# Linear attention and a GELU layer on one core: loads issued as slots come free, x in token order with whole-tile stores, and one step fewer transposed by DMA

## The chip, the cores and the metric

One core of a Trainium2 chip runs the whole program. The metric is the time on the device in microseconds (us); for the kernel before, three timed runs are shown, and one further execution was profiled. TensorE (PE) multiplies matrices, VectorE (DVE), ScalarE (ACT) and GpSimd (POOL) do elementwise work, and SyncE (SP) issues nearly all DMAs, one after the other, from one queue.

## The reference

The first half is block-wise linear attention with a decay lam per head: q, k and v are (4, 8, 768, 64), that is batch, heads, tokens and head width. The second half takes the attention's output as x, 3072 tokens by 512, through a layer with a tanh GELU.

```python
for b in range(nb):                      # blocks of 64 tokens
    intra = einsum('bhic,bhjc->bhij', qb, kb) * Dmask     # lam**(i-j) for i >= j, else 0
    intra = einsum('bhij,bhjd->bhid', intra, vb)
    inter = einsum('bhid,bhde->bhie', qb * lam_pow, kv_state)
    out[:, :, sl] = intra + inter
    kv_state = lam_block * kv_state + einsum('bhsd,bhse->bhde', kb * rev_pow, vb)
x = out.transpose(0, 2, 1, 3).reshape(3072, 512)
h = x @ w_in                             # 512 x 2048
g = 0.5 * h * (1 + tanh(c * (h + 0.044715 * h**3)))
return g @ w_out                         # 2048 x 512
```

## The kernel before

**Steps.** The attention is cut into 24 steps. A pair of steps covers 256 tokens of one batch entry (a super block, `sb`, three for each batch entry), and each step of the pair covers four of the eight heads. Inputs and weights are cast to fp16 on the chip.

**Loads.** `load_step(s)` (L60) issues three loads of 256 KB each, of q, k and v, from the SyncE queue (L67). Partition p of a tile holds the tokens 2p and 2p + 1, next to each other, so a load moves long rows. The tiles come from a pool of five slots for each of q, k and v; a load waits until the cast of an older step has freed a slot. At the top of the program the steps 0 to 3 are put on the queue, then the weights (L78, L84), mixed with steps 4 and 5, then steps 6 to 11. From step 8 of the loop on, `load_ahead(n + 4)` adds one step at a time.

**Casts.** `prep(s)` (L180) multiplies q by its decay on DVE (L195), casts k on ACT (L200) and multiplies v by the inverse decay on POOL (L201). The attention needs q and k with the head width on partitions. Up to step 7 TensorE transposes them, in `stage_t(s)`: eight products with an identity (L217) into PSUM, and a copy out of it (L221 on ACT for steps 1 to 3, else L223 on DVE). From step `FIRST_DMA_T` on, `prep` issues a DMA transpose instead (L205), on SyncE's queue too, and `stage_t` does nothing.

**Regions.** `region(n, s)` (L235) is TensorE's part of the attention. For step n it makes the scores (Sps, L255) and the products of k and v that feed the state (L268); DVE multiplies the scores by the mask (PT, L289). For step s = n - 1 it adds the masked scores times v (L304) and the state times q (L314), in PSUM (OK). ACT then copies the result into xT (L322), which holds x transposed: channels on partitions, tokens along the row. `update` makes the new state on DVE (L341, L344) and a block-diagonal copy of it on POOL (u, L348).

In PSUM the 128 columns of one half (c) of a super block stand as j, t: first the tokens of one parity, then those of the other, because a partition held two neighbouring tokens. xT keeps that order. A token tile of the second half's output therefore comes out with partitions 0 to 63 for the even rows and 64 to 127 for the odd ones, and it is stored in two pieces:

```python
for j in range(2):
    pin(nc.sync.dma_start(out=dst[j], in_=o32[half64(j), :]))
...
return out[row0 : row0 + P, :].rearrange("(p j) e -> j p e", j=2)
```

**The second half** is cut into pieces, which `queue_group(g)` (L361) puts on a list, `filler`. `mm1` multiplies xT by w_in (Hps, L373, four or eight products with four passes over the channels) and ACT applies the GELU (gT, L375). `mm2` multiplies gT by a quarter of w_out (O2ps, L384, four products of 512 columns); after the fourth quarter DVE copies the tile to SBUF (L391) and SyncE stores it (L393). There are seven groups of one or two super blocks. `fill(n)` takes n pieces off the list, so that TensorE has work between the regions. `mm2_last` makes the last tile, in two column ranges, and stores them from SyncE and ACT (L410).

**Order.** `pin` keeps the instructions of each engine in the order of the program text; that order is written out by hand. Up to step 7 it is a list of calls (L449 to L509), afterwards a loop. `idle(n)` (L426) issues n products of 128 by 512 on ones whose result nobody reads. The waits between engines follow from the tiles that they share.

Of the kernel before, what the change touches and what calls it, by code (L numbers as in the profile page):

```python
# [15 lines left out]
def kernel(  # L16
# [10 lines left out]
    nc = tc.nc  # L27
# [8 lines left out]
    NF = DFF // P  # L36
    NC = DM // P
    NSTEP = B * NSB * 2
    FIRST_DMA_T = 8
    PSUM = bass.MemoryType.PSUM  # L40

    const = ctx.enter_context(tc.tile_pool(name="const", bufs=1))
# [71 lines left out]
    load_wout(2)  # L114
    load_wout(3)
    load_step(5)
    for s in range(6, 12):
        load_step(s)

    def load_ahead(s):  # L120
# [35 lines left out]
    def square(i):  # L156
        pin(nc.vector.tensor_tensor(sq[i + 1][:], sq[i][:], sq[i][:], ALU.mult))
# [22 lines left out]
    def prep(s):  # L180
        half = s % 2
        q32, k32, v32 = ld32.pop(s)
        hs = slice(half * HH, (half + 1) * HH)

        def wide(t):
            return t.rearrange("p j h d -> p h j d")

        def decay(t):
            return t[:, hs, :].unsqueeze(3).to_broadcast([P, HH, 2, D])

        tqk = a16p.tile([P, 2, 2, HH, D], FP16, tag="qk16", name=f"qk16_{s}")
        tq, tk = tqk[:, 0], tqk[:, 1]
        tv = a16p.tile([P, 2, HH, D], FP16, tag="v16", name=f"v16_{s}")
        q_eng = nc.gpsimd if s == 3 else nc.vector
        pin(q_eng.tensor_tensor(wide(tq), q32[:], decay(dq), ALU.mult))  # L195
        if s == 0:
            inverse(halves[0])
            odd(halves[1])
            inverse(halves[1])
        pin(nc.scalar.activation(out=wide(tk), in_=k32[:], func=AF.Copy))  # L200
        pin(nc.gpsimd.tensor_tensor(wide(tv[:]), v32[:], decay(dv), ALU.mult))  # L201
        a16[s] = (tq, tk, tv)
        if s >= FIRST_DMA_T:
            o = qkp.tile([P, 2, 2, 2, P], FP16, tag="qkT", name=f"qkT_{s}")
            pin(nc.sync.dma_start_transpose(out=o[:].rearrange("p a j h t -> p (a j h) t"),  # L205
                                            in_=tqk[:].rearrange("p a j h d -> p (a j h d)")))
            qkT[s] = o

    def stage_t(s):
        if s >= FIRST_DMA_T:  # L210
# [21 lines left out]
    def half64(i):  # L232
        return slice(64 * i, 64 * i + 64)

    def region(n, s, split=False):  # L235

        OK = [ps_M.tile([P, 512], FP32, tag="M", name=f"OK{c}") for c in range(2)]
        opened = set()

        def start(c, hl):  # L240
            if (c, hl) in opened:
                return False
            opened.add((c, hl))
            return True

        if n is not None:
            o = qkT[n]
            _, tk, tv = a16[n]
            Sps = ps_S.tile([P, 2, 2, 2, P], FP32, tag="S", name="Sps")

            def scores():
                for hp in range(2):
                    for jk in range(2):
                        for hl, c in TILES:
                            pin(nc.tensor.matmul(  # L255
                                Sps[half64(c), hl, hp, jk, :],
                                o[half64(hl), 1, jk, hp, half64(c)],
                                o[half64(hl), 0, :, hp, half64(c)], start=True, stop=True,
                                skip_group_check=True))

            def products():
                last = (n // 2) % NSB == NSB - 1
                for jk in range(2):
                    for hp in range(2):
                        for c, hl in TILES:
                            if c == 1 and last:
                                continue
                            pin(nc.tensor.matmul(  # L268
                                OK[c][half64(hl), 256 + hp * D : 256 + hp * D + D],
                                tk[half64(c), jk, 2 * hp + hl, :],  # L270
                                tv[half64(c), jk, 2 * hp + hl, :],
                                start=start(c, hl), stop=(jk == 1), skip_group_check=True))
                Kps[n] = OK

            if split:
                products()
                update(n, 0)
                scores()
            else:
                scores()  # L280
                products()
            PT = []
            for hps in ([slice(0, 1), slice(1, 2)] if split else [slice(0, 2)]):
                w = hps.stop - hps.start
                t = ptp.tile([P, 2, w, 2, P], FP16, tag=f"PT{w}", name=f"PT_{n}_{hps.start}")
                for src, dst in ([(Sps[:, :, hps.start], t[:, :, 0])] if split else
                                 [(Sps[:].rearrange("p a b c d -> p (a b) c d"),
                                   t[:].rearrange("p a b c d -> p (a b) c d"))]):
                    pin(nc.vector.tensor_tensor(  # L289
                        dst.rearrange("p a c d -> p a (c d)"),  # L290
                        src.rearrange("p a c d -> p a (c d)"),
                        mask[:].unsqueeze(1).to_broadcast([P, 2 * w, 2 * P]), ALU.mult))
                PT += [t[:, :, i] for i in range(w)]
            PTs[n] = PT
        if s is None:
            return
        sbg, half = divmod(s, 2)
        o = qkT.pop(s)
        PT = PTs.pop(s)
        _, _, tv = a16.pop(s)  # L300
        for hp in range(2):
            for jk in range(2):
                for c, hl in TILES:
                    pin(nc.tensor.matmul(  # L304
                        OK[c][half64(hl), hp * P : hp * P + P], tv[half64(c), jk, 2 * hp + hl, :],
                        PT[hp][half64(c), hl, jk, :], start=start(c, hl), stop=False,
                        skip_group_check=True))
        ins = ins_of.pop(s)
        for c in range(2):
            u = ins[c]  # L310
            if u is None:
                continue
            for hp in range(2):
                pin(nc.tensor.matmul(OK[c][:, hp * P : hp * P + P], u[:, hp].rearrange("p l d -> p (l d)"),  # L314
                                     o[:, 0, :, hp, half64(c)], start=False, stop=True,
                                     skip_group_check=True))
        g, i = group_of[sbg]
        if g not in xT:
            xT[g] = xtp.tile([P, NC, len(groups[g]) * SB], FP16, tag="xT", name=f"xT_{g}")
        dst = xT[g][:, 2 * half : 2 * half + 2, i * SB : (i + 1) * SB]  # L320
        for c in range(2):
            pin(nc.scalar.activation(  # L322
                out=dst[:, :, c * P : (c + 1) * P],
                in_=OK[c][:, 0:256].rearrange("p (hp m) -> p hp m", hp=2), func=AF.Copy))

    ins_of = {}

# [33 lines left out]
    def queue_group(g):  # L361
# [18 lines left out]
        def mm2(tau, part):  # L380
            if part == 0:
                O2[tau] = ps_M.tile([P, DM], FP32, tag="M", name="O2ps")
            for f in range(4 * part, 4 * part + 4):
                pin(nc.tensor.matmul(O2[tau][:], gT[:, f, tau * P : (tau + 1) * P],  # L384
                                     w_out16[:, f, :], start=(f == 0), stop=(f == NF - 1)))
            if part < 3:
                return
            o2 = O2.pop(tau)
            dst = rows(tau)
            o32 = otp.tile([P, DM], FP32, tag="o32", name="o32")  # L390
            pin(nc.vector.tensor_copy(out=o32[:], in_=o2[:]))  # L391
            for j in range(2):
                pin(nc.sync.dma_start(out=dst[j], in_=o32[half64(j), :]))  # L393

        def rows(tau):
            row0 = groups[g][0] * SB + tau * P
            return out[row0 : row0 + P, :].rearrange("(p j) e -> j p e", j=2)

        def mm2_last(tau):
            dst = rows(tau)  # L400
            o32 = otp.tile([P, DM], FP32, tag="o32", name="o32")
            for lo, hi in ((0, 384), (384, DM)):
# [4 lines left out]
                                         stop=(f == NF - 1)))  # L407
                pin(nc.vector.tensor_copy(out=o32[:, lo:hi], in_=o2[:]))
                for j, eng in ((0, nc.sync), (1, nc.scalar)):
                    pin(eng.dma_start(out=dst[j][:, lo:hi], in_=o32[half64(j), lo:hi]))  # L410

        for f in range(0, NF, per):
            filler.append(lambda f=f: mm1(f))
# [18 lines left out]
    def fill(n):  # L432
        for _ in range(min(n, len(filler))):
            filler.pop(0)()
# [14 lines left out]
    idle(12)  # L449
    prep(0)  # L450
    stage_t(0)
    square(5)
    square(6)
    prep(1)
# [1 line left out]
    idle(2)  # L456
    R(0, None)
    stage_t(1)
    idle(2)
    U(0)  # L460
    prep(2)
    R(1, 0)
    stage_t(2)
    idle(3)
    U(1)
# [23 lines left out]
    prep(5)  # L489
    fill(4)  # L490
    stage_t(5)
    fill(2)
    R(5, 4)
    U(5)
    prep(6)
    fill(2)
    stage_t(6)
    fill(2)
    R(6, 5)
    U(6)  # L500
    prep(7)
    fill(2)
    stage_t(7)
    prep(8)
    fill(2)
    R(7, 6)
    U(7)
# [3 lines left out]
    for n in range(8, NSTEP + 1):  # L511
        m = n if n < NSTEP else None
        if m is not None:
            load_ahead(n + 4)
            stage_t(n)
        if n + 2 < NSTEP:
            prep(n + 2)
# [39 lines left out]
```

## Time and profile before

| | |
|---|---|
| timed runs | 222.67, 221.65, 222.20 us, median 222.2 |
| profiled execution | 219.72 us, of which the span from first to last instruction is 217.9 |
| TensorE busy | 205.9 us (94%), 2105 products |
| DVE, ACT, POOL busy | 91.7, 91.8, 64.9 us |
| mean granted TensorE clock | 0.981 |
| DMA | 38.08 MB, mean 175 GB/s |
| SyncE's issues | 72 loads of 256 KB, 8 of weights, 46 stores of 128 KB, 16 transposes |

The page cuts the span into 40 equal slices of 5.45 us; a digit is the busy share of an engine in that slice, in tenths, and for PEclk the clock that TensorE was granted. The chain of work that ended last is followed back from the last instruction, at each step to what released it. The groups give, for a line and an operation, the count, the busy time and the mean duration, and the idle time of the engine ahead of them with what ended it.

### The profile page before, as it was taken

To read this page: it belongs to the slowest core of one execution; us is meant where nothing else is said; L and a number is where in the kernel's file an instruction comes from. 1 tells how busy PE (TensorE), PEld (TensorE's weight loads), DVE (VectorE), ACT (ScalarE), POOL (GpSimd) and SP (SyncE) were. 2 spreads that over 40 slices of the span, in tenths; PEclk is the share of its full clock that TensorE was granted. 3 is DMA by queue.
4 is the path that set the end of the run, shared out by engine and by line. 5 is a ranking of instruction groups with operands and counts; after the bars stand their busy time and mean duration, and the time that the engine had idled before them with its cause. 6 is when DMAs were issued, how large, how long until landed. Compare 5 with 4: busy or idle time off the path is not lost.

```text
span 217.9 us, 5061 instructions
## 1 busy us (share of the span) xinstructions
PE 205.9 (94%) x2105; PEld 107.6 (49%) x2105; DVE 91.7 (42%) x178; ACT 91.8 (42%) x175; POOL 64.9 (30%) x82
## 2 busy tenths in 40 slices
PE   7699999999939999999999999999999999999993
PEld 2264444555825686444454544544554454444452
DVE  4778612587722642634526621445730251100121
ACT  2375665323823266177701277620377310466000
POOL 5494146634724432124224203403410110000000
PEclk9969999999979999999999999999999999999998
DMA  5999999999989869499943969744330023200223
GB/s 139 300 335 390 385 345 376 288 297 294 293 190 241 146 168 250 114 228 195 293 101 77 225 183 215 183 96 101 79 70 0 0 51 78 68 3 0 46 50 96
DMA packets 63303, 38.08 MB, mean 175 GB/s; under 512 B 19120, under 2 KB 56240, under 8 KB 63280
## 3 DMA queue, kind: packets, MB, share of 16 engines
q1 hardware_dynamic: 63120, 37.63, 67.5%
q8 instruction: 16, 0.26, 0.5%
q10 hardware_dynamic: 160, 0.13, 0.2%
q14 instruction: 7, 0.06, 0.1%
HBM read 27.27 MB, written 6.29 MB: 154 GB/s over the span
## 4 chain that ended last, share of the span: by engine, by line
PE 86%; DMA 4%; POOL 3%; DVE 2%; ACT 2%; SPq 1%; issue 1%; DVEq 0%; POOLq 0%
PE Hps L373 38%; PE O2ps L384 35%; PE Sps L255 4%; PE OK L314 3%; DMA v<-in_v_dram 3%; PE OK L304 3%; PE O2ps L405 2%; DMA qkT<-qk 2%; PE Tps L217 1%; POOL u L348 1%; SPq L67 1%; PE OK L268 1%; POOL v L201 1%; DVE PT L289 1%; DVE qk L195 1%
## 5 line engine op out<-in xcount | busy, mean ns | idle before, releaser
L373 PE MATMUL Hps<-xT,w_in 128*128 128x512 f16 (+1 forms) x448 | 86.5, 351 | 0.2 <-ACT xT L322 0.2
L384 PE MATMUL O2ps<-w_out,gT 128*128 128x512 f16 x368 | 82.9, 379 | 0.0
L375 ACT ACTIVATE gT<-Hps 128x512 f16<-128x512 f32 x96 | 57.2, 597 | 36.4 <-PE Hps L373 35.5
L373 PEld LDWEIGHTS <-w_in 128*128 128x128 f16 x448 | 43.8, 99 | 38.3 <-issue 0.5
L348 POOL TENSOR_TENSOR u<-t,lumask 128x256 f16<-128x256 f32 x40 | 28.7, 728 | 97.7 <-DVE t L344 66.0
L384 PEld LDWEIGHTS <-gT 128*128 128x128 f16 x368 | 35.4, 98 | 39.7
L289 DVE TENSOR_TENSOR PT<-Sps,mask 128x1024 f16<-128x1024 f32 (+1 forms) x25 | 29.4, 1180 | 50.4 <-PE Sps L255 50.4
L322 ACT ACTIVATE xT<-OK 128x256 f16<-128x256 f32 x48 | 15.9, 381 | 59.8 <-PE OK L314 43.3
L391 DVE COPY o<-O2ps 128x512 f32<-128x512 f32 x23 | 15.8, 690 | 53.5 <-PE O2ps L384 50.7
L201 POOL TENSOR_TENSOR v<-v,dv 128x512 f16<-128x512 f32 x24 | 25.8, 1079 | 3.8 <-DMA v<-in_v_dram 2.3
L195 DVE TENSOR_TENSOR qk<-q,dq 128x512 f16<-128x512 f32 x23 | 20.4, 893 | 6.3 <-DMA q<-in_q_dram 6.3
L200 ACT ACTIVATE qk<-k 128x512 f16<-128x512 f32 x24 | 14.9, 626 | 7.1 <-DMA k<-in_k_dram 7.1
L344 DVE SCALAR_TENSOR_TENSOR t<-t,lamu,OK 128x64 f32<-128x64 f32 x64 | 14.5, 275 | 1.6 <-PE OK L268 0.6
L255 PE MATMUL Sps<-qkT 64*64 64x128 f16 x384 | 10.4, 228 | 4.8 <-DMA qkT<-qk 3.5
L255 PEld LDWEIGHTS <-qkT 64*64 64x64 f16 x384 | 6.4, 110 | 14.4 <-issue 7.0
L304 PE MATMUL OK<-PT,v 64*64 64x128 f16 x384 | 10.7, 226 | 0.0
L430 PE MATMUL idle<-ones 128*128 128x512 f16 x25 | 8.7, 488 | 1.5 <-DVE ones L126 1.5
L103 POOL CAST w_out<-wo 128x1024 f16<-128x1024 f32 x6 | 6.6, 1115 | 10.6 <-DMA wo<-in_moe_w_out_dram 10.6
L314 PE MATMUL OK<-qkT,u 128*128 128x128 f16 x80 | 8.8, 226 | 0.0
L268 PE MATMUL OK<-v,qk 64*64 64x64 f16 x320 | 7.3, 196 | 0.8 <-POOL v L201 0.8
L304 PEld LDWEIGHTS <-v 64*64 64x64 f16 x384 | 7.2, 112 | 0.9 <-issue 0.8
L217 PE MATMUL Tps<-ident,qk 128*128 128x128 f16 x64 | 5.9, 232 | 1.3 <-DVE qk L195 0.6
(34 smaller groups left out, 51.1 us busy)
## 6 DMA issues: line engine op xcount, KB each, us to landing
q<-in_q_dram SPq DMA_DIRECT2D x24, 256.0 KB, 4.5
k<-in_k_dram SPq DMA_DIRECT2D x24, 256.0 KB, 4.7
v<-in_v_dram SPq DMA_DIRECT2D x24, 256.0 KB, 5.1
out_dram<-o SPq DMA_DIRECT2D x46, 128.0 KB, 2.4
wi<-in_moe_w_in_dram SPq DMA_DIRECT2D x4, 1024.0 KB, 10.2
wo<-in_moe_w_out_dram SPq DMA_DIRECT2D x4, 1024.0 KB, 8.8
qkT<-qk SPq DMA_TRANSPOSE x16, 3.9
out_dram<-o SPq DMA_DIRECT2D x1, 96.0 KB, 2.1
```

Of the source, the lines that this page charges most:

```text
L195: pin(q_eng.tensor_tensor(wide(tq), q32[:], decay(dq), ALU.mult))
L201: pin(nc.gpsimd.tensor_tensor(wide(tv[:]), v32[:], decay(dv), ALU.mult))
L255: pin(nc.tensor.matmul(Sps[half64(c), hl, hp, jk, :], o[half64(hl), 1, jk, hp, half64(c)], o[half64(hl), 0, :, hp, half64(c)], start=True, ...
L289: pin(nc.vector.tensor_tensor(dst.rearrange("p a c d -> p a (c d)"), src.rearrange("p a c d -> p a (c d)"), mask[:].unsqueeze(1).to_broadc ...
L304: pin(nc.tensor.matmul(OK[c][half64(hl), hp * P : hp * P + P], tv[half64(c), jk, 2 * hp + hl, :], PT[hp][half64(c), hl, jk, :], start=star ...
L314: pin(nc.tensor.matmul(OK[c][:, hp * P : hp * P + P], u[:, hp].rearrange("p l d -> p (l d)"), o[:, 0, :, hp, half64(c)], start=False, stop ...
L322: pin(nc.scalar.activation(out=dst[:, :, c * P : (c + 1) * P], in_=OK[c][:, 0:256].rearrange("p (hp m) -> p hp m", hp=2), func=AF.Copy))
L348: pin(nc.gpsimd.tensor_tensor(bd[:], t[:].unsqueeze(2).to_broadcast([P, 2, 2, D]), lumask[:, 2 * half : 2 * half + 2, :].unsqueeze(3).to_b ...
L373: pin(nc.tensor.matmul(Hps[:, i, :], w_in16[:, c, f * P : (f + 1) * P], x[:, c, :], start=(c == 0), stop=(c == NC - 1)))
L375: pin(nc.scalar.activation(out=gT[:, f0 : f0 + per, :], in_=Hps[:], func=AF.Gelu_apprx_tanh))
L384: pin(nc.tensor.matmul(O2[tau][:], gT[:, f, tau * P : (tau + 1) * P], w_out16[:, f, :], start=(f == 0), stop=(f == NF - 1)))
L391: pin(nc.vector.tensor_copy(out=o32[:], in_=o2[:]))
```

## The change

- `FIRST_DMA_T` goes from 8 to 9: step 8 is transposed on TensorE and copied out by DVE, steps 9 to 23 by DMA.
- At the top only steps 0 to 8 are loaded. From step 6 on, `prep(s)` ends with the loads of step s + 3, behind its casts and its transpose; the loop's own `load_ahead(n + 4)` goes.
- ACT writes xT in token order: it reads j, t from PSUM and writes t, j. The rows of an output tile are then 128 neighbouring rows, and a tile is one store of 256 KB. In `mm2_last` each of the four stores takes 64 neighbouring rows.
- `prep(6)`, `prep(7)` and `prep(8)` stand earlier in the list of calls, and three calls of `idle` are added or made longer, five products in all.

```diff
-    FIRST_DMA_T = 8
+    FIRST_DMA_T = 9
...
-    for s in range(6, 12):
+    for s in range(6, 9):
         load_step(s)
...
             qkT[s] = o
+        if s >= 6:
+            load_ahead(s + 3)
...
             pin(nc.scalar.activation(
-                out=dst[:, :, c * P : (c + 1) * P],
-                in_=OK[c][:, 0:256].rearrange("p (hp m) -> p hp m", hp=2), func=AF.Copy))
+                out=dst[:, :, c * P : (c + 1) * P].rearrange("p hp (t j) -> p hp j t", j=2),
+                in_=OK[c][:, 0:256].rearrange("p (hp j t) -> p hp j t", hp=2, j=2),
+                func=AF.Copy))
...
-            for j in range(2):
-                pin(nc.sync.dma_start(out=dst[j], in_=o32[half64(j), :]))
+            pin(nc.sync.dma_start(out=dst, in_=o32[:]))
...
-            return out[row0 : row0 + P, :].rearrange("(p j) e -> j p e", j=2)
+            return out[row0 : row0 + P, :]
...
-                    pin(eng.dma_start(out=dst[j][:, lo:hi], in_=o32[half64(j), lo:hi]))
+                    pin(eng.dma_start(out=dst[half64(j), lo:hi], in_=o32[half64(j), lo:hi]))
...
     stage_t(0)
+    idle(1)
...
     stage_t(1)
-    idle(2)
+    idle(5)
     U(0)
     prep(2)
     R(1, 0)
+    idle(1)
     stage_t(2)
...
     stage_t(5)
+    prep(6)
     fill(2)
     R(5, 4)
     U(5)
-    prep(6)
     fill(2)
     stage_t(6)
+    prep(7)
     fill(2)
     R(6, 5)
     U(6)
-    prep(7)
-    fill(2)
+    fill(1)
+    prep(8)
+    fill(1)
     stage_t(7)
-    prep(8)
     fill(2)
     R(7, 6)
...
         if m is not None:
-            load_ahead(n + 4)
             stage_t(n)
```

## The prediction

> **What bounds the kernel now.** I read the head of the page first, then its slices, then a table of stages, then the chain of work that ended last.
>
> ```profile
> span 217.9 us, 5061 instructions
> PE 205.9 (94%) x2105; PEld 107.6 (49%) x2105; DVE 91.7 (42%) x178; ACT 91.8 (42%) x175; POOL 64.9 (30%) x82
> PE   7699999999939999999999999999999999999993
> PEclk9969999999979999999999999999999999999998
> ```
>
> TensorE is busy 94% of the span and no other engine passes 49%, so only time in which TensorE idles or runs slowed can be won. The slices (5.45 us each) show where that is: the first two, the twelfth (3 tenths, about 60 us, the clock down to 7 behind it) and the last. The table of stages gives sizes (stretch, its length, busy time of PE, PEld, DVE, ACT and POOL, granted clock, DMA share, GB/s).
>
> ```profile
> 60.00:63.46 3.46, 0.00 (x0) 0.00 (x0) 0.00 (x0) 0.56 (x1) 1.50 (x2) 0.91 0.86 180
> 63.46:70.90 7.44, 7.44 (x86) 4.71 (x90) 2.84 (x6) 2.42 (x5) 2.63 (x3) 0.81 1.05 233
> 70.90:214.40 143.50, 143.50 (x1384) 73.14 (x1384) 51.75 (x91) 59.01 (x116) 28.37 (x36) 1.00 0.52 116
> ```
>
> From 70.90 to 214.40 TensorE never idles, at clock 1.00: nothing that the change does to loads and stores there can help, it can only hurt. The hole from 60.00 to 63.46 and the lower clock behind it are what can be won. The chain in order of time (start, length, work) says what the hole is:
>
> ```profile
> 53.15 0.62 PE Tps L217 x8
> ...
> 55.52 0.35 PE Sps L255 x16
> ...
> 56.43 3.51 PE Hps L373 x32
> 60.05 3.37 DMA qkT<-qk
> 63.46 0.64 PE Sps L255 x15
> ...
> 65.08 2.37 PE Hps L373 x16
> 67.45 3.45 PE O2ps L384 x16
> ```
>
> TensorE waits for the DMA transpose of step 8, the first one made by DMA. Why that starts only at 60.05 is read from SyncE's queue, DVE and ACT:
>
> ```profile
> 53.43 0.78 SPq L67 DMA_DIRECT2D v<-in_v_dram  x1
> 54.26 5.61 SPq L393 DMA_DIRECT2D out_dram<-o  x8
> 60.05 2.77 SPq L205 DMA_TRANSPOSE qkT<-qk  x2
> 54.41 0.70 DVE L195 TENSOR_TENSOR qk<-q,dq 128x512 f16<-128x512 f32 x1
> 51.53 1.15 ACT L200 ACTIVATE qk<-k 128x512 f16<-128x512 f32 x2
> ```
>
> These casts are step 8's q (done at 54.41 + 0.70 = 55.11) and the k of steps 7 and 8 (done at 52.68). The transpose could have gone at 55.1. It stood behind the last of the twelve loads that are put on the queue at the top, and behind eight half-tile stores.
>
> **The change, part by part.**
>
> *Step 8 back on TensorE (FIRST_DMA_T 9).* The hole goes:
>
> ```profile
> PE Sps L255 <- DMA qkT<-qk: 3.5, 1, 3.5
> PE Tps L217 <- DVE qk L195: 0.4, 1, 0.4
> ```
>
> Minus 3.5 us (first row; the columns are total, times, longest). With it goes the half clock behind it. A region and the 16 Hps products after it take 63.46 to 67.45, 3.99 us. The same region at 55.52 was through at 56.43, 0.91, and 16 of the 32 Hps products there take 1.75: 2.66 together. So minus 1.3 us. In exchange TensorE makes eight transposes, 0.62 us by the row of 53.15: plus 0.6. DVE copies their result out of PSUM (0.69 us, the 43.10 row below) while TensorE has the two filler pieces, 16 Hps products or 1.75 us, that `fill(2)` puts between `stage_t(8)` and the scores: nothing on the path, and 0.7 if that cover were gone.
>
> *`prep` of steps 6, 7 and 8 moved forward.* Each is a cast on DVE (q), ACT (k) and POOL (v), and DVE's order decides.
>
> ```profile
> 43.10 0.69 DVE L223 COPY qkT<-Tps 128x1024 f16<-128x1024 f16 x1 [1.30 <-PE Tps L217]
> 45.43 1.22 DVE L289 TENSOR_TENSOR PT<-Sps,mask 128x1024 f16<-128x1024 f32 x1
> 46.94 0.68 DVE L195 TENSOR_TENSOR qk<-q,dq 128x512 f16<-128x512 f32 x1
> 52.38 0.72 DVE L195 TENSOR_TENSOR qk<-q,dq 128x512 f16<-128x512 f32 x1
> 57.86 1.74 DVE L195 TENSOR_TENSOR qk<-q,dq 128x512 f16<-128x512 f32 x2
> L67 SPq DMA_DIRECT2D k<-in_k_dram x1: 1927/1927/1927, 38.2 to 38.2; - x1
> DMA to landing us min/median/max: 6.1/6.1/6.1
> DMA to landing us min/median/max: 3.1/4.9/9.4
> ```
>
> q6 goes from 46.94 to behind the copy at 43.10, so DVE reaches it at 43.8. Its load must be there: k6 was issued at 38.2 and landed 6.1 later (the first two figures of landing are this one load and all loads), at 44.3, and q6 stands one place ahead of it. It runs before PT at 45.43, for which 0.9 us stay. The copy of step 6 then has one cast less ahead of it than before. q7 goes from 52.38 to behind that copy, and q8 takes its place at 52.38; the store's copy (0.69) and the copy of step 7 follow, done at 54.5 for scores at 55.52 - 0.4 = 55.1: 0.6 to spare. q9 ends 0.4 before 58.73 (half of the last DVE row), the copy of step 8 about 59.0; the scores of step 8 come at 63.46 - 3.5 - 0.4 + 0.6 = 60.2. So none waits. The gain is the wait of step 7's transposes for their own q cast, the second wait row above: minus 0.4, since that cast now lies a step ahead. What it costs if q6's load takes the longest landing seen, 9.4 in place of 6.1: 3.3 less the 1.5 us of room just named (0.9 and 0.6), 1.8.
>
> *Loads.* SyncE meets loads 9, 10 and 11 one `prep` at a time, the last two behind three stores. Each load is now issued three steps ahead of its cast, 22 us at the 7.44 of the stage table, where the slowest landed in 9.4: nothing. In the loop it stands behind the step's transpose instead of ahead of it; TensorE waits for neither there: nothing.
>
> *Stores.* 23 whole stores in place of 46 halves, which took 0.70 each (5.61 for eight). A whole one costs SyncE between 0.70 and two halves, 1.40; a 256 KB load took 0.78, so near the lower end: four of them about 3. Off the path, and 2.5 us earlier for what follows on the queue, with 0 as the other bound. The stores after the last product keep number and size: nothing.
>
> *Step 9's transpose* is what is late next. Its queue is free about 57.5 (60.05 less 2.5), its q cast ends about 58.3, and its scores come at 70.90 - 4.6 = 66.3 if the sum below holds. The transposes of this trace landed in (least, median, longest):
>
> ```profile
> DMA to landing us min/median/max: 3.0/3.9/6.1
> L322 ACT ACTIVATE xT<-OK 128x256 f16<-128x256 f32 x48 | 15.9, 381 | 59.8 <-PE OK L314 43.3
> L169 DVE COPY lumask<-sq 64x4 f32<-64x4 f32 x2 | 0.3, 160 | 0.0
> L170 DVE TENSOR_TENSOR lamu<-lumask 128x4 f32<-128x4 f32 x1 | 0.2, 162 | 0.0
> ```
>
> So it is there between 61.3 and 64.4: in time by 1.9 us at worst.
>
> *xT in token order.* The 48 copies on ACT (381 ns each) will write every second element. No ACT row of this trace writes so. The nearest, though far off, is DVE's copy into every second element of lumask, 160 ns, against 162 for an operation as wide without gaps. I take 381 unchanged. Bounds: 0 and a doubling. A doubled pair, 1.5 us, would still lie under the eight O2ps products (half of 3.45, 1.73) that follow the region ahead of every group but the first, and show there alone, 0.8 us. [...]
>
> *Five more idle products* (1, 3 and 1) in the opening.
>
> ```profile
> 14.89 1.01 POOL qk L195
> 11.29 0.42 PE L255 MATMUL Sps<-qkT 64*64 64x128 f16 x16 [0.68 <-ACT qkT L221]
> 11.70:15.00 3.30, 3.30 (x60) 0.50 1.13 326
> ```
>
> From 10 to 15.9 us the chain runs through POOL's casts and state tiles (the last of them is the first row), not through TensorE. The three have the shape of the O2ps products, 3.45 / 16 = 0.22 each, 0.65 in a wait of 0.68 (second row). Taken: 0; bounds 0 and 0.4, the one ahead of step 2's transposes at half clock. For the same reason nothing is gained if the half clock of the third row goes.
>
> **The sum.** 3.5 + 1.3 + 0.4 - 0.6 = 4.6 us less. The profiled execution took 219.72 us, its span 217.9: 215.1 and 213.3. It lies 2.5 under the median of the runs, 222.2, and the saving comes off that: **217.6 us**, 2.1% less.
>
> [...] In the rows half clock follows 3.5 us without a product, and stands for 3.30 us in the opening. [...]
>
> **Rivals.**
>
> [...]
>
> *B, the wait moves to step 9.* If its transpose goes as late as in the trace, second after 60.05, about 61.5, and takes the longest 6.1, it lands at 67.6 against 66.3: 1.3 us lost, too short to halve the clock, 218.9. With loads 10 and 11 slow on the queue besides, it stands where step 8 stood, 3.5 and 1.3: 222.4, no change. Against: queue and casts are both early.
>
> *C, slower: the interleaved ACT write.* Each copy takes t. Before six of the seven groups a pair hides under 1.73 us; beyond t = 0.86 each waits 2(t - 0.86), and the first group 2(t - 0.38). At t = 1.3 that is 5.3 + 1.8 = 7.1: 224.7. It decides against the change from t = 1.2, three times the row. Against: the lumask row.
>
> **How the numbers follow.** The forecast 0.69; a late q6, A, or B's short form, all near 219, 0.17; B in full 0.08; C 0.06. Half a per cent, 1.1 us, is about what a measurement of this kernel tells from no change. So faster 0.86, same 0.08, slower 0.06. The range is 215.2 to 219.8: at the lower end the 2.5 us by which the runs lie above the profiled execution, were they a wait that goes too; at the upper A (219.2), B's short form and the late q6 (219.4), with 0.4 for the idles. B in full and C stay outside.
>
> **What would show it.** Right: no hole in the twelfth slice, clock 1.00 from 60 to 71, eight more transposes ahead of step 8's scores near 60.2, no score product waiting for qkT, xT at about 381 ns, the end some 3.5 us after the last product as now. Wrong: scores of step 9 waiting near 66, DVE idle for q near 44, xT above 0.86 us, or half clock between 15 and 20.

## The result, and the profile after

The changed kernel takes 214.81 us in the median (214.72 to 215.29), the kernel before 221.93 in the runs beside it (221.14 to 222.67): a ratio of 0.968, with a 95% interval of 0.965 to 0.972. That is 7.1 us less, where 4.6 were forecast (217.6), and just under the range, which ended at 215.2. The profiled execution of after took 215.29 us, its span 213.5; the forecast for these was 215.1 and 213.3. So the working fits the two profiles and misses the runs, and the question is why. On another chip the same two kernels took 221.36 and 214.88 us (e13 below), 6.5 us less. Ratios are taken over the fast runs of both kernels alone, which in e5 to e8, where single runs of before were down at 218.3 and 218.7, leaves out the slower half of its 23 runs.

The head of the page of after, and its slices (5.34 us each):

```profile
span 213.5 us, 5059 instructions
PE   7879999999999999999999999999999999999993
PEclk9999999999999999999999999999999999999999
```

The twelfth slice has no hole, and the clock is full throughout (mean 1.000). The chain of after where the hole was (start, length, work):

```profile
58.08 0.45 PE Tps L219 x8
58.52 1.75 PE Hps L376 x16
60.27 0.35 PE Sps L257 x16
...
62.93 3.45 PE O2ps L387 x16
66.39 0.35 PE Sps L257 x16
```

Step 8 is transposed on TensorE at 58.08, its scores start at 60.27 (forecast 60.2) and those of step 9 at 66.39 (66.3), with nothing but products in between. Step 9's DMA transpose, issue and landing, and the group of the xT copies:

```profile
58.64 1.71 SPq L205 DMA_TRANSPOSE qkT<-qk  x1
DMA to landing us min/median/max: 4.7/4.7/4.7
L324 ACT ACTIVATE xT<-OK 128x256 f16<-128x256 f32 x48 | 18.3, 451 | 51.3 <-PE OK L316 39.5
```

It landed at 63.3, 3 us ahead of its scores. An xT copy took 451 ns instead of 381.

### The profile page after: what moved, and what is told of

It is laid out like the page before. It is cut to its first block, busy times and chain, and to the rows that moved or that the text cites. A ratio compares the mean times of both kernels' runs of the same rounds, so it can differ in the third digit from the quotient of the medians.

```text
span 213.5 us, 5059 instructions
## 1 busy us (share of the span) xinstructions
PE 205.1 (96%) x2118; PEld 107.0 (50%) x2118; DVE 91.3 (43%) x179; ACT 94.2 (44%) x175; POOL 64.2 (30%) x82
## 3 DMA queue, kind: packets, MB, share of 16 engines
q1 hardware_dynamic: 61696, 37.37, 63.4%
## 4 chain that ended last, share of the span: by engine, by line
PE 86%; DMA 7%; SPq 2%; ACT 2%; DVE 1%; issue 0%; ACTq 0%
PE Hps L376 38%; PE O2ps L387 34%; DMA k<-in_k_dram 7%; PE Sps L257 3%; PE OK L316 3%; PE OK L306 3%; SPq L67 2%; PE O2ps L407 2%; PE Tps L219 1%; PE OK L270 1%; ACT qkT L223 1%; ACT xT L324 1%; ACT qk L200 1%; DVE PT L291 0%; PE idle L432 0%
## 5 line engine op out<-in xcount | busy, mean ns | idle before, releaser
L376 PEld LDWEIGHTS <-w_in 128*128 128x128 f16 x448 | 43.3, 98 | 38.1 <-issue 0.6
L351 POOL TENSOR_TENSOR u<-t,lumask 128x256 f16<-128x256 f32 x40 | 27.9, 706 | 91.1 <-DVE t L347 64.2
L324 ACT ACTIVATE xT<-OK 128x256 f16<-128x256 f32 x48 | 18.3, 451 | 51.3 <-PE OK L316 39.5
L195 DVE TENSOR_TENSOR qk<-q,dq 128x512 f16<-128x512 f32 x23 | 19.7, 859 | 6.9 <-DMA q<-in_q_dram 6.9
L432 PE MATMUL idle<-ones 128*128 128x512 f16 x30 | 10.2, 479 | 1.5 <-DVE ones L126 1.5
L306 PE MATMUL OK<-PT,v 64*64 64x128 f16 x384 | 10.2, 218 | 0.0
L219 PEld LDWEIGHTS <-qk 128*128 128x128 f16 x72 | 4.6, 99 | 5.0 <-DVE qk L195 1.8
```

What stands on the lines that cost most here:

```text
L306: pin(nc.tensor.matmul(OK[c][half64(hl), hp * P : hp * P + P], tv[half64(c), jk, 2 * hp + hl, :], PT[hp][half64(c), hl, jk, :], start=star ...
L324: pin(nc.scalar.activation(out=dst[:, :, c * P : (c + 1) * P].rearrange("p hp (t j) -> p hp j t", j=2), in_=OK[c][:, 0:256].rearrange("p ( ...
L351: pin(nc.gpsimd.tensor_tensor(bd[:], t[:].unsqueeze(2).to_broadcast([P, 2, 2, D]), lumask[:, 2 * half : 2 * half + 2, :].unsqueeze(3).to_b ...
L376: pin(nc.tensor.matmul(Hps[:, i, :], w_in16[:, c, f * P : (f + 1) * P], x[:, c, :], start=(c == 0), stop=(c == NC - 1)))
```

## The experiments

**Where the missing 2.5 us are.** Three theories were set against each other with the kernel before itself, and with single parts of the change.

*e1: the kernel before, a second profile.* No edit.

> The kernel before, unchanged, for a second profile. The timed runs of before lie some 2 us above its one profiled execution (219.72), those of after do not lie above theirs. Theory 1 (the half clock of the opening lies or lasts differently in the usual execution and delays the chain there): a time of 221.5 to 222.7, and in the profile or in the mean clock of the runs a longer or later half clock before 21 us, so that the first GELU products start near 22 to 23 us instead of 20.8. Theory 2 (the hole at step 8 is usually longer): the same time, the opening as before, and a hole of about 5.5 us instead of 3.5 at 60 us. Theory 3 (a constant part outside the span): the time minus the span is 4 us instead of 1.8.

222.51 us in the profiled execution, median 221.99. The eight half stores on its SyncE queue, its chain at step 8, and the wait:

```profile
54.31 7.00 SPq L393 DMA_DIRECT2D out_dram<-o  x8
...
61.49 3.42 DMA qkT<-qk
64.91 0.04 issue
64.95 0.64 PE Sps L255 x15
...
66.56 3.41 PE Hps L373 x16
69.98 3.72 PE O2ps L384 x16
73.69 0.35 PE Sps L255 x16
...
PE Sps L255 <- DMA qkT<-qk: 4.6, 1, 4.6
```

The hole is 4.6 us instead of 3.5. The landing took what it took before (3.42 and 3.37 us); the transpose was issued later, behind stores that held the queue for 7.00 us instead of 5.61, one of them alone for 1.96. Why that store took so long is not shown. And the 16 Hps products behind the hole take 3.41 us, where they took 2.37 in the first profile and 1.75 at full clock. Time less span is 1.8 us as before, so theory 3 falls. Theory 2 named the right place, but the hole alone is shorter than it said. The span is 2.8 us longer: 1.1 in the hole, 1.3 in the longer half clock (8.74 us from step 8's scores to step 9's, against 7.44), and 0.4 ahead of step 5's scores (45.17 against 44.79).

*e2: before with the five idle products.*

```diff
     stage_t(0)
+    idle(1)
...
     stage_t(1)
-    idle(2)
+    idle(5)
...
     R(1, 0)
+    idle(1)
```

> Before, with only the five added idle products. Theory 1: they keep the clock up in the opening, about 2 us less than before, 219.5 to 220. Theory 2: no change, 222 (0 to 0.4 us more). Theory 3: no change.

221.16 us, ratio 0.996 (0.992 to 1.000): at most a trace of what theory 1 needed. Nor is there a longer half clock in the opening: over the first 21 us the granted clock is 1.00 in e1 and in e2, and 0.92 in the first profile of before.

*e3: before with step 8 on TensorE.*

```diff
-    FIRST_DMA_T = 8
+    FIRST_DMA_T = 9
```

> Before, with only FIRST_DMA_T 9. Loads, stores, idles and the order of prep as before. By the sum of the prediction the hole and the half clock behind it go and the eight transposes come: 3.5 + 1.3 - 0.6 = 4.2 us less. Theory 1: 217.5 to 218, as the opening stays. Theory 2: the longer hole goes whole, 215 to 215.5. A rival on the transpose of step 9: it stays behind the same loads and eight half stores, goes at 60.1 and lands at 63 to 66, scores of step 9 wanted at 66.5: no new wait, or up to 1 us.

215.63 us against 221.13 in the runs of before beside it, ratio 0.973 (0.970 to 0.975): 5.5 to 6 of the 7 us come from this one number. Step 9's transpose stood behind all loads and eight half stores and was still in time:

```profile
61.08 1.36 SPq L205 DMA_TRANSPOSE qkT<-qk  x1
DMA to landing us min/median/max: 3.2/3.2/3.2
...
66.90 0.35 PE Sps L255 x16
```

It landed at 64.3, and its scores came at 66.90.

*e4: after without the five idle products* (the edit of e2 taken back).

> After, without the five added idle products. Theory 1: about 2 us above after, 216.8 to 217.3, with half clock in the opening of the profile. Theory 2: as after, 214.8, whatever the opening's clock does, since POOL carries the chain there.

214.86 us, as after. The idles are worth nothing, and theory 1 falls with them.

**How much of it is the clock.** *e7: before, TensorE kept busy while it waits.*

```diff
         fill(a)
+        if n == 8:
+            idle(16)
         R(m, n - 1)
```

> Before, with sixteen idle products (3.5 us) ahead of the region that takes step 8's scores, so that TensorE multiplies while it waits for the transpose. The wait stays. Theory (half clock behind the hole costs 1.3 us in the first profile and about 2.5 in the usual execution): clock 1.00 behind the wait, 218.5 to 219.5. Rival (the usual execution differs by a longer hole alone, half clock costs 1.3 or less): 220 to 221.

219.84 us in the median of 12 runs, against 221.50 in the 23 runs of before beside them. That lies between the two forecasts, and the ratio, 0.998 (0.993 to 1.002), settles nothing. The granted clock does: its mean is 0.997 to 1.000 in eleven of the twelve runs (0.992 in the other), where 21 of the 23 runs of before have 0.992 or less. The chain of e7:

```profile
61.10 3.33 DMA qkT<-qk
64.43 0.04 issue
64.47 0.42 PE Sps L255 x16
...
65.46 1.75 PE Hps L373 x16
67.20 3.45 PE O2ps L384 x16
70.66 0.35 PE Sps L255 x16
```

*e16: before, a third profile,* run later to see which length of half clock is the usual one.

> The kernel before once more, for a third profile. [...]

221.75 us, span 219.9, with the transpose landing where it did in e7:

```profile
54.74 6.18 SPq L393 DMA_DIRECT2D out_dram<-o  x8
...
61.11 3.41 DMA qkT<-qk
64.52 0.04 issue
64.56 0.64 PE Sps L255 x14
...
66.17 3.27 PE Hps L373 x16
69.44 3.45 PE O2ps L384 x16
72.90 0.35 PE Sps L255 x16
...
PE Sps L255 <- DMA qkT<-qk: 4.3, 1, 4.3
```

From step 8's scores to step 9's: 8.34 us here, 6.19 in e7 with the same wait and the clock up (mean 1.000). Half clock costs 2.2 us; the spans, 219.9 and 217.7, differ by the same 2.2. The granted clock of TensorE in stretches of 1 us (stretch, length, busy, clock, DMA share, GB/s), first in e16, then in the first profile of before:

```profile
62.00:63.00 1.00, 0.00 (x0) 0.67 0.80 163
63.00:64.00 1.00, 0.00 (x0) 0.50 0.91 169
...
68.00:69.00 1.00, 1.00 (x7) 0.50 1.18 236
69.00:70.00 1.00, 1.00 (x7) 0.92 1.27 143
```

```profile
62.00:63.00 1.00, 0.00 (x0) 0.91 0.90 177
...
65.00:66.00 1.00, 1.00 (x7) 0.50 1.10 332
66.00:67.00 1.00, 1.00 (x10) 0.89 0.93 246
```

Half clock lasted from 62.3 to 69.2 in e16, 6.8 us, and from 62.8 to 66.2 in the first profile, 3.4. Of four profiles with this hole (the two, e1 and e2) three have the long one. What fixes which of the two lengths comes is not shown, and was not separated from the hole's own length: holes of 3.4 (e5) and 3.5 us had the short one, of 3.8 (e2), 4.3 and 4.6 the long one.

Which of the two is usual can be read from the mean granted clock, which is on record for runs without a profile too. It is 0.983 or 0.984 in the profiles e1, e2 and e16, with the long half clock, and 0.989 to 0.992 in e5, e8 and e12, with the short one. Of the 81 runs of before for which it is on record, 45 have 0.989 to 0.992 and took 220.2 to 221.8 us; 34 have less and took 221.7 to 223.4; two have more and took 218.3 and 218.7. So, read this way, the long half clock is no more usual than the short one, and the three profiles in four overstate it. What sets the first profile apart is its short hole. (Its own mean, 0.981, also holds the 3.30 us of half clock in the opening.)

**What holds the transpose of step 8.** *e5: before with token order and whole stores* (the xT copy, `rows` and the stores as in the change).

> Before, with only x in token order and one store for a tile; step 8 still transposed by DMA, loads as before. [...] Rival (what holds the transpose are the loads ahead of the stores, or its casts): it goes at 60 as before, 221 to 222. The copies into xT take 451 ns as in after instead of 381, hidden.

220.15 us, ratio 0.999 (0.995 to 1.003). With four whole stores ahead of it, which held the queue for 2.45 us where the eight halves of the first profile took 5.61, the transpose went 2 us earlier than there, and landed hardly earlier:

```profile
58.03 5.70 DMA qkT<-qk
```

That is 5.7 us to landing, at 63.7, with a hole of 3.4 us. In e7, on the same chip, it went at 61.10 and landed 3.3 us later, at 64.4. So 3.1 us on the queue brought 0.7 at the landing. (Next to the favourable first profile, with 60.05 and 63.4, they would seem to bring nothing.) The medians, 220.15 and 221.50, leave room for a small gain, which the ratio does not show. So what stands ahead of the transpose on SyncE's queue is not all that holds it. That what the DMA engines still have to move counts too fits the trace: in the two microseconds from 58 to 60 they moved 399 and 351 GB/s in e5, and from 61 to 63 in e16, on another chip, whose transpose went at 61.11, 160 and 163. It was not tested by itself.

*e9: before with only the loads moved.*

```diff
-    for s in range(6, 12):
+    for s in range(6, 9):
...
+        if s >= 6:
+            load_ahead(s + 3)
...
-            load_ahead(n + 4)
```

> Before, with only the loads moved: steps 9 to 11 no longer at the top, step s + 3 behind the casts of step s. Half-tile stores, prep order and FIRST_DMA_T 8 as before. The transpose of step 8 goes ahead of load 11, near 57.5. Theory (what stands ahead of it, in SyncE's queue or still moving in the DMA engines, sets when it lands: 5.7 us behind load 11 and four stores in the kernel with whole stores, 3.4 in before): 4 to 5.5 us to landing, at 61.5 to 63, a hole of 1.5 to 3 us, half clock in part of the executions: 216.5 to 220. Rival (3.4 us to landing wherever it is issued): lands at 61, hole of 1 us, 215.5 to 216.5. Rival (the loads have no part in it): as before, 221 to 222.

216.47 us, ratio 0.979 (0.976 to 0.983). Chain and wait:

```profile
56.25 5.21 DMA qkT<-qk
...
PE Sps L257 <- DMA qkT<-qk: 1.1, 1, 1.1
```

With load 11 behind the transpose it lands at 61.5, the hole is 1.1 us, and the clock stays up in this execution (mean 1.000; two of the six runs have a mean of 0.992, and what they looked like is not shown). So the loads' new place by itself is worth 4.7 us, 221.19 to 216.47, two thirds of the whole change, on the same hole.

*e6: after with step 8 by DMA* (FIRST_DMA_T 8).

> After, with FIRST_DMA_T 8 again: loads, stores and prep order of after, but step 8 transposed by DMA. Theory: the transpose now stands ahead of load 11 and of the last store of the first group, goes near 54 to 55 and lands near 58 to 60, scores wanted near 59.8; the eight transposes on TensorE (0.45 us on the chain of after) are saved: 214.3 to 214.9, no half clock. Rival (a DMA transpose there is late whatever the queue, since the engines are full of loads): a hole of 1 to 3 us, 216 to 220.

215.31 us, no better than after (214.81).

```profile
53.53 6.37 DMA qkT<-qk
...
PE Sps L257 <- DMA qkT<-qk: 0.5, 1, 0.5
```

The transpose went at 53.53 and needed 6.37 us; a wait of 0.5 us remained, about what the saved transposes (0.45) give.

*e8: after with steps 7 and 8 by DMA* (FIRST_DMA_T 7).

> After, with FIRST_DMA_T 7: steps 7 and 8 transposed by DMA too. The transpose of step 7 stands behind load 9 and three stores, which in after end at 52.0, so it lands at 55.5 to 58 against scores wanted near 54.9: a hole of 0.6 to 3 us, less 0.9 for sixteen transposes saved on TensorE: 214.5 to 217. Rival (transposes by DMA are free once loads queue behind casts): 213.9 to 214.3.

215.75 us in the median, two of six at 217.4 to 217.7. In the profile (one of these two) step 7's transpose made a hole of 1.9 us and half clock followed:

```profile
PE Sps L257 <- DMA qkT<-qk: 1.9, 1, 1.9
...
57.20 5.16 PE Hps L376 x32
```

32 Hps products take 5.16 us instead of 3.51. So half clock (0.50 from 57.2 to 60.6) came here behind a hole shorter than the 3.5 us of the first profile. The two runs at 217.4 and 217.7 us have a mean clock of 0.989 and 0.988, the four at 215.5 to 215.8 one of 0.997 to 1.000: by that mean the quicker ones had no half clock of this length.

*e12: the same kernel, a second profile.*

> The kernel with FIRST_DMA_T 7 a second time, for another profile. Its executions fell into two groups, 217.4 to 217.7 and 215.5 to 215.8; the profiled one was of the upper, with a hole of 1.9 us and half clock for 3.4 us behind it. [...] Rival: the lower group has no hole, since the transpose lands earlier.

218.17 us, with a hole of 2.8 us and half clock (0.50 from 56.9 to 60.3): the upper group again. Whether the lower group, at full clock, has the same hole or none stays open.

**What the order of prep is worth.** *e10: after, with the three calls of prep where they stood before.*

> After, with prep(6), prep(7) and prep(8) where they stood before. Step 7's transposes wait for their q cast again (0.36 us in before) and step 6's too (0.1): 0.4 to 0.6 us more than after, 215.2 to 215.4. Rival (the 0.8 us between the kernel with step 8 on TensorE alone and after come from stores and loads): no change, 214.8.

216.23 us, 1.4 above after, but on another chip. *e13 and e14: after and the kernel of e10, on one chip.*

> After, unchanged, as the yardstick of this set: 214.6 to 215.0. If the order of prep counts for more than its waits on TensorE, the next kernel stays 1.0 us or more above this one; if the 1.4 us seen before came with the chip, both move together.

> After with the old places of prep(6) to prep(8), beside after itself. Its profile had step 9's scores 0.4 us later than after, and 0.5 us more behind the last product. Theory (the order is worth the two waits of the q casts): 0.4 us above the after of this set. Rival (it is worth 1.4 us): 1.0 us or more above it.

214.88 and 216.27 us. From the scores of step 5 to those of step 7, e14 first, then e13:

```profile
45.58 0.35 PE Sps L257 x16
...
53.95 0.62 PE Tps L219 x8
...
56.32 0.35 PE Sps L257 x16
```

```profile
45.13 0.35 PE Sps L257 x16
...
55.00 0.35 PE Sps L257 x16
```

10.74 against 9.87 us: 0.87 for the order, and not the 0.4 of the longer wait. Twice 0.17 of it is in the transposes: eight take 0.62 behind a wait and 0.45 in a running stream (58.08 in after). The rest are the waits for the q casts of steps 6 and 7 (0.37 for step 7). The two profiled executions differ by 1.9 us, as e14's, at 216.77, was the slowest of its six: 0.45 of that lies ahead of step 5's scores. The last 0.6 us stand behind the last copy out of PSUM, which is 3.9 us from the end in e14 (210.83 + 0.29 to 215.0) and 3.3 in e13. e10 has 3.8 there too, and e3, with the same order of prep, 3.2. Nothing in the edit explains that, and it stays open. So of the 1.4 us that the order is worth in after, 0.87 is traced.

*e15: after, with step 5's q and k ahead of the last load of w_out, and ACT's part of that cast behind step 5's.*

```diff
     load_wout(2)
-    load_wout(3)
-    load_step(5)
+    load_step(5, "qk")
+    load_wout(3)
+    load_step(5, "v")
...
-    cast_wout(3)
+    cast_wout(3, (0,))
...
     prep(5)
+    cast_wout(3, (1,))
```

> After, with step 5's q and k loaded ahead of the last 1 MB of w_out, and ACT's part of that cast behind step 5's k cast. In after TensorE waits from 42.37 to 43.42 in two parts (0.54 and about 0.1 besides the transposes of q) for step 5, whose k landed 9.1 us after its issue. Theory (that wait is what is left of the loading phase): scores of step 5 0.5 to 0.9 us earlier, 214.0 to 214.4. Rival (the weights now land too late for the fourth quarter of the O2ps products, near 43.8): no gain or 0.5 us more.

214.62 us (214.34 to 215.36) against 214.88 (214.65 to 214.96): not to be told apart.

## Why the prediction was right and wrong

- *The place and the cause of the loss*: right, as far as they went. Hole and half clock at step 8 carry the result (e3, e7), and nothing behind step 9 changed.
- *The size of the hole, "minus 3.5", and of the half clock, "minus 1.3"*: these are the terms that failed. They were read from one execution, and it was a favourable one. The hole is 3.8 us in e2, 4.3 in e16 and 4.6 in e1, because the transpose is issued later behind the same eight half stores. The half clock costs 1.3 to 1.7 us where it is short (first profile, e5) and 2.2 to 2.6 where it is long (e16, e2, e1).
- *The sum, done again on one chip.* From e16 to e13 the scores of step 5 stand still (45.07 and 45.13), those of step 7 come 0.8 us earlier by the order of prep (forecast 0.4), those of step 8 another 3.9 (the hole of 4.3 less 0.45 for the transposes, forecast 0.6), and those of step 9 another 2.2 by the half clock: 6.9, and the times lie 6.9 apart (221.75 and 214.88). e16 is one of the executions with the long half clock; the medians there lie 6.5 apart.
- *"The saving comes off that" (the median)*: the wrong step of the argument. The 2.5 us between the first profile and the runs were seen and treated as fixed, with their loss only as the lower end. From the first profile to e16 the time grows by 2.0, of which 0.8 is the hole, 0.9 the half clock, and 0.3 lies ahead of step 5. So most of the gap was the two terms themselves, and went with the hole. After has no such spread: 214.7 to 215.3.
- *The fit of the two profiles* (215.1 forecast, 215.29 measured) is in part luck: in the profile of after, step 5's scores come 0.75 us later than in the first profile of before (45.54 and 44.79), which hides the 0.4 to 0.5 by which the order of prep gained more than forecast. In the lower end of the range is a slip of 0.1: 217.6 less 2.5 is 215.1.
- *"The transpose could have gone at 55.1"*: half right. It could go, but an earlier issue brought the landing forward by less: issued at 53.53 it needed 6.37, at 56.25 5.21, at 58.03 5.70, at 60.05 3.37.
- *Loads and stores, priced at nothing on the path*: right beside step 8 on TensorE. e3 has neither; it lies 0.8 us above e4, about what the order of prep alone gains. With step 8 left to DMA the loads' new place is worth 4.7 us (e9).
- *"Too short to halve the clock"*, of rival B's wait of 1.3 us: the first 1.45 us of the span of before, without a product, have clock 1.00, and e9's hole of 1.1 us left the clock up (mean 1.000), but e8's 1.9 did not (0.50 from 57.2). What a wait of 1.3 us in mid-stream would do was not shown.
- *Step 9's transpose*: in time, by 3 us. Rival B did not occur, even in e3 with the old queue.
- *xT*: 451 ns instead of 381, 18% more where no change was taken, hidden as the bounds had it, and far from the 1.2 us of rival C. Besides the writes to every second element the same edit made the rows that a copy walks through shorter, 64 elements instead of 128, so which of the two costs it is not shown.
- *A, whose 219.2 stands in the range and in the chances*: 1.6 us, half of 3.3, for a half clock of the opening that lies at 15.0 to 18.3 instead of 11.7 to 15.0. No run shows it. In its place the profiles show none in the opening of e1, e2 and after, 1.00 over the first 21 us, against 0.92 in the first of before.
- *The idles*: nothing, as priced (e2, e4).

## What to carry to other kernels

A profile is one execution. Where its time lies outside the spread of the timed runs, take a second one before pricing a stall: here most of the gap was the stall itself, which was longer in other executions. The mean granted clock of the runs without a profile then said how often each case came. TensorE's hole at step 8 cost its length and then the half clock behind it, 1.3 to 2.6 us for holes of 3.4 to 4.6; filling the wait with idle products (e7) removed the second part alone, and showed it: a mean clock of 0.997 to 1.000 in eleven of twelve runs. And where DMAs queue, look at what is still being moved as well as at what is still to be issued: behind the same loads and the same bytes to store, an issue 3.1 us earlier landed 0.7 us earlier (e5 and e7), which fits that reading and was no test of it.

## What the runs showed of the hardware

- Half clock followed holes of 1.9 (e8), 2.8 (e12) and 3.4 us (e5), not one of 1.1 (e9). In e8 it began near 57.2, some 0.9 us after TensorE was at work again, and lasted to 60.6. In every profile where it followed a hole it lasted 3.4 us (first profile of before, e5, e8, e12) or 6.8 (e1, e2, e16).
- The DMA transpose of step 8 needed between 3.3 (e7) and 6.4 us (e6) to landing: 3.3 to 3.4 behind eight half stores that held the queue for 5.6 to 7.0 us (before, e1, e2, e7, e16), and 5.7 behind two loads and four whole stores issued within 4.2 us (e5).
- The same eight transposes took 0.62 us behind a wait and 0.45 without one.
